# Rebuilding the attention half of a fused relu²-attention and feed-forward kernel on array tiles, with relu on ScalarE and the square on VectorE

## The chip, the cores and the metric

The kernel runs on one core of one Trainium2 chip. The metric is the device time of one execution in microseconds (us). A kernel was run several times; the time quoted is the median. The profile is a record of one execution, and its span is a microsecond or two below the time.

TensorE does matrix products, ScalarE and VectorE bring results out of PSUM (the banks that TensorE writes) into SBUF, GpSimd converts types and issues some of the loads, and SyncE issues the others. In the profile they are PE (PEld for its weight loads), ACT, DVE, POOL and SP.

## The reference

```python
# q, k, v: (8 batches, 12 heads, 448 positions, 64)
scores = q @ k.T / sqrt(64)
attn   = maximum(scores, 0)**2 / 448
x      = (attn @ v) -> (3584 tokens, 768)        # heads side by side
h      = x @ w_in                                # w_in  768 x 2048
out    = maximum(h, 0)**2 @ w_out                # w_out 2048 x 768, out float32
```

The inputs are float32; both kernels compute in fp16 with float32 sums.

## The kernel before

It works through 48 head pairs. For each pair it transposes q and k, computes scores for two heads, applies relu², and multiplies with v. The hidden and output matmuls of earlier batches are kept in a queue, and `fill` puts some of them between the attention matmuls, so that TensorE has work while it waits. A head has only 64 dimensions, but the array is 128 x 128. The kernel pads: q sits in one half of the rows with zeros in the other, and v in one half of the columns with zeros beside it.

```python
ps_p   = tile_pool("ps",   bufs=4, PSUM)   # hidden, scores AND attention-times-V share these
psmi_p = tile_pool("psmi", bufs=2, PSUM)   # transposes
pso_p  = tile_pool("pso",  bufs=1, PSUM)   # output, 768 columns

def relu2_psum_to_sbuf(dst, src, n):            # src is PSUM, read by both engines
    sq = sq_p.tile([P, S], FP16)
    nc.scalar.activation(out=sq[:n], in_=src[:n], func=AF.Square)
    nc.vector.scalar_tensor_tensor(out=dst[:n], in0=src[:n], scalar=0.0, in1=sq[:n],
                                   op0=ALU.is_gt, op1=ALU.mult)     # (src > 0) * sq

# transposes: float32, 4 x 112 rows for q and as many for k, each followed by fill(224)
    nc.tensor.transpose(tq[:, i*SB:(i+1)*SB], qst[:, i], ident)
# ... eviction to qTA (upper half zero), qTB (lower half zero) and kT
# scores: contraction over 128 rows, 64 of them zeros
    for c in range(4):
        for j, qT in ((0, qTA), (1, qTB)):
            nc.tensor.matmul(sps, lhsT=kT[:, c*P:(c+1)*P], rhs=qT, start=True, stop=True)
            relu2_psum_to_sbuf(at, sps, P);  fill(448)
# attention times V: 128 output columns, of which 64 are this head's
    for c in range(4):
        for j in range(2):
            nc.tensor.matmul(avps, lhsT=(vA if j == 0 else vB)[:, c, :], rhs=aa[2*c+j], ...)
            fill(448)
# ... weights are loaded piece by piece, one piece after each head pair of batch 0
```

## Time and profile before

The time was 539.67 us (median of two runs, 539.41 to 539.94).

| what | value | view |
|---|---|---|
| TensorE busy | 498.5 of 538.1 us, 93% | table of busy times |
| VectorE, ScalarE busy | 373.7 us, 297.8 us | table of busy times |
| share of TensorE in the chain that ended last | 87% | chain of waits |
| step of a 448-column matmul | 0.189 us | timeline, start to start |
| third four-head unit's last V matmul | 64.4 us | timeline |

These lines come from the page of the profile before: the span, the busy times of each engine, and three rows that cut the span into 40 equal slices of 13.5 us. A digit is a busy share in tenths; PEclk is the clock that TensorE was granted.

```profile
span 538.1 us, 8018 instructions
...
PE 498.5 (93%) x2816; PEld 281.6 (52%) x2816; DVE 373.7 (69%) x663; ACT 297.8 (55%) x589; POOL 138.5 (26%) x220
...
PE   1675999999999999999999999999999999999886
...
PEclk9979899999999999999999999999999999999999
DMA  9999534544355454343445454343545552100211
```

From the fifth slice on TensorE is at nine tenths or more, until the last three. In the first four the DMA engines are full and TensorE is not. That is batch 0, where the queue has no hidden or output matmuls to fill with.

The next lines are from the timeline of TensorE before, in a dense stretch. The columns are the start (us), the time from the first start to the last end (us), the engine, the line, the operation, output and inputs, the shape of the stationary operand, the shapes of output or moving data, and how many instructions the row joins.

```profile
200.04 0.35 PE L131 MATMUL hps<-xt_119,w_1_97 128*128 128x448 f16 x1
200.23 0.35 PE L236 MATMUL avps<-at_2416,vf_132 128*128 128x448 f16 x1
...
202.69 0.26 PE L217 MATMUL tk<-ident,kst 112*128 112x112 f32 x1
202.79 0.35 PE L131 MATMUL hps<-xt_118,w_0_96 128*128 128x448 f16 x1
...
207.10 0.38 PE L158 MATMUL ops<-w_0_102,g_2451 128*128 128x512 f16 x1
207.31 0.27 PE L162 MATMUL ops<-w_0_102,g_2451 128*128 128x256 f16 x1
207.42 0.35 PE L227 MATMUL sps_2545<-qTA,kT 128*128 128x448 f16 x1
```

Read starts, not durations. A matmul is recorded with 0.35 us, but the next one starts 0.19 us after it (200.04 to 200.23), since they are pipelined. A scores or V matmul with half its rows or columns zero costs the same step as a full one. Averaged over the dense part of the trace, the steps are 0.189 us for 448 columns, 0.215 and 0.109 us for the output pair (512 and 256 columns), and 0.097 us for a float32 transpose.

### The profile page before, as it was taken

Reading aid. Unit: us, or ns where it says so; the run is one execution under the profiler, and the core shown is the slowest. Engines: PE = TensorE matmul, PEld = TensorE weight load, DVE = VectorE, ACT = ScalarE, POOL = GpSimd, SP = SyncE. Lnnn points to the kernel's source line nnn. Section 1 sums busy time; section 2 is a strip of 40 time slices with the busy share of each in tenths; the row PEclk is TensorE's granted clock in tenths of the full one; section 3 lists DMA queues with packets and bytes.
Section 4 is the critical chain, followed back from the end, with each engine's and each line's share of the span. In section 5 each row is a group of like instructions: output and inputs, shape, how many; then the busy total and the mean of one; then the engine's idle time right before and its main releaser. Section 6 shows DMA issues by size and latency. Waiting matters only on the chain.

```text
span 538.1 us, 8018 instructions
## 1 busy us (share of the span) xinstructions
PE 498.5 (93%) x2816; PEld 281.6 (52%) x2816; DVE 373.7 (69%) x663; ACT 297.8 (55%) x589; POOL 138.5 (26%) x220
## 2 busy tenths in 40 slices
PE   1675999999999999999999999999999999999886
PEld 1332455555555555555555555555555555554553
DVE  2676898888887667898875667898875667764000
ACT  0444576667675546676745546676754555654111
POOL 7453311331133122113232123213232113000000
PEclk9979899999999999999999999999999999999999
DMA  9999534544355454343445454343545552100211
GB/s 160 201 204 197 82 51 70 83 84 92 61 86 94 88 119 69 45 78 48 86 85 108 89 120 65 48 75 46 80 93 92 107 108 37 10 0 3 86 60 59
DMA packets 142408, 45.36 MB, mean 84 GB/s; under 512 B 135968, under 2 KB 138016, under 8 KB 142368
## 3 DMA queue, kind: packets, MB, share of 16 engines
q1 hardware_dynamic: 93120, 33.04, 24.9%
q0 software_dynamic: 49248, 11.81, 22.5%
q8 instruction: 22, 0.36, 0.3%
q14 instruction: 18, 0.15, 0.1%
HBM read 45.61 MB, written 11.01 MB: 105 GB/s over the span
## 4 chain that ended last, share of the span: by engine, by line
PE 87%; DMA 7%; ACT 3%; SPq 1%; DVE 1%; issue 1%; ACTq 0%
PE hps L131 27%; PE ops L158 18%; PE avps L236 13%; PE ops L162 9%; DMA kst<-in_k_dram 6%; PE tq L208 3%; PE tk L217 3%; ACT osb L169 2%; DMA qst<-in_q_dram 2%; ACT sq L113 1%; SPq L189 1%; SPq L193 1%; DVE at_527 L114 0%; DVE at_588 L114 0%; DVE at_612 L114 0%
## 5 line engine op out<-in xcount | busy, mean ns | idle before, releaser
L113 ACT ACTIVATE sq<-hps 128x448 f16<-128x448 f32 x128 | 69.4, 542 | 58.2 <-PE hps L131 57.1
L197 POOL DMA_DIRECT2D vf_130<-in_v_dram x24 | 18.4, 768 | 159.6 <-PE avps L236 126.0
L197 POOL DMA_DIRECT2D vf_134<-in_v_dram x24 | 18.4, 768 | 146.3 <-PE avps L236 144.9
L227 PEld LDWEIGHTS <-kT 128*128 128x128 f16 x384 | 36.8, 100 | 32.3 <-issue 4.9
L169 ACT ACTIVATE osb<-ops 128x768 f32<-128x768 f32 x28 | 22.8, 813 | 51.3 <-PE ops L162 51.3
L210 DVE TENSOR_SCALAR qTA<-tq 64x448 f16<-64x448 f32 x48 | 29.2, 608 | 29.6 <-PE tq L208 29.6
L208 PE MATMUL tq<-ident,qst 112*128 112x112 f32 x192 | 33.0, 269 | 15.5 <-DMA qst<-in_q_dram 13.8
L131 PE MATMUL hps<-xt_122,w_4_100 128*128 128x448 f16 x128 | 45.1, 352 | 0.0
L131 PE MATMUL hps<-xt_120,w_2_98 128*128 128x448 f16 x128 | 45.1, 352 | 0.0
L131 PE MATMUL hps<-xt_121,w_3_99 128*128 128x448 f16 x128 | 45.1, 352 | 0.0
L131 PE MATMUL hps<-xt_123,w_5_101 128*128 128x448 f16 x128 | 45.1, 352 | 0.0
L131 PE MATMUL hps<-xt_119,w_1_97 128*128 128x448 f16 x128 | 45.1, 352 | 0.0
L131 PE MATMUL hps<-xt_118,w_0_96 128*128 128x448 f16 x128 | 45.0, 352 | 0.0
L217 PE MATMUL tk<-ident,kst 112*128 112x112 f32 x192 | 35.5, 273 | 8.4 <-DMA kst<-in_k_dram 8.4
L208 PEld LDWEIGHTS tq<-ident,qst 112*128 112x128 f32 x192 | 25.1, 147 | 25.5 <-issue 11.9
L219 DVE TENSOR_SCALAR kT<-tk 128x448 f16<-128x448 f32 x48 | 29.9, 623 | 11.0 <-PE tk L217 9.8
L217 PEld LDWEIGHTS tk<-ident,kst 112*128 112x128 f32 x192 | 25.1, 149 | 15.9 <-issue 10.1
L212 DVE TENSOR_SCALAR qTB<-tq 64x448 f16<-64x448 f32 x48 | 30.1, 628 | 1.5
L131 PEld LDWEIGHTS <-w_5_101 128*128 128x128 f16 x128 | 12.5, 97 | 13.5 <-issue 3.1
L197 POOL DMA_DIRECT2D vf_136<-in_v_dram x24 | 18.7, 779 | 2.9 <-DMA w_5_101<-in_moe_w_in_dram 1.5
L197 POOL DMA_DIRECT2D vf_132<-in_v_dram x24 | 18.8, 782 | 0.0
L131 PEld LDWEIGHTS <-w_2_98 128*128 128x128 f16 x128 | 12.5, 97 | 11.6
(1910 smaller groups left out, 1368.4 us busy)
## 6 DMA issues: line engine op xcount, KB each, us to landing
qst<-in_q_dram SPq DMA_DIRECT2D x96, 112.0 KB, 2.7
kst<-in_k_dram SPq DMA_DIRECT2D x96, 112.0 KB, 2.7
out_dram<-osb SPq DMA_DIRECT2D x28, 384.0 KB, 2.8
vf_130<-in_v_dram POOLq DMA_DIRECT2D x24, 48.0 KB, 2.5
vf_132<-in_v_dram POOLq DMA_DIRECT2D x24, 48.0 KB, 2.9
vf_134<-in_v_dram POOLq DMA_DIRECT2D x24, 48.0 KB, 2.6
vf_136<-in_v_dram POOLq DMA_DIRECT2D x24, 48.0 KB, 2.8
w_0_96<-in_moe_w_in_dram POOLq DMA_DIRECT2D x1, 512.0 KB, 6.1
```

Of the source, the lines that this page charges most:

```text
L113: nc.scalar.activation(out=sq[:n], in_=src[:n], func=AF.Square)
L131: nc.tensor.matmul(hps[0], lhsT=w1[m][:, f * P : (f + 1) * P], rhs=xt[m][:, b * S : (b + 1) * S], start=(m == 0), stop=(m == NDMT - 1),)
L158: nc.tensor.matmul(ops[0][:, 0:512], lhsT=gt[f][:, rs], rhs=w2[f][:, 0:512], start=(f == 0), stop=(f == NFFT - 1),)
L162: nc.tensor.matmul(ops[0][:, 512:768], lhsT=gt[f][:, rs], rhs=w2[f][:, 512:768], start=(f == 0), stop=(f == NFFT - 1),)
L169: nc.scalar.activation(out=osb, in_=ops[0], func=AF.Copy, scale=CO)
L197: nc.gpsimd.dma_start(out=vt[:, 0:3, j * 64 : j * 64 + 64], in_=v[b, 2 * hp + j, 0:384].rearrange("(c p) d -> p c d", p=P),)
L208: nc.tensor.transpose(tq[:, i * SB : (i + 1) * SB], qst[:, i], ident)
L212: nc.vector.tensor_scalar(out=qTB[64:128, :], in0=tq[64:128, :], scalar1=1.0, scalar2=None, op0=ALU.mult)
L217: nc.tensor.transpose(tk[:, i * SB : (i + 1) * SB], kst[:, i], ident)
L219: nc.vector.tensor_scalar(out=kT[:, 0:448], in0=tk, scalar1=SK, scalar2=None, op0=ALU.mult)
L227: nc.tensor.matmul(sps, lhsT=kT[:, c * P : (c + 1) * P], rhs=qT, start=True, stop=True)
L236: nc.tensor.matmul(avps, lhsT=(vA if j == 0 else vB)[:, c, :], rhs=aa[2 * c + j], start=(c == 0 and j == 0), stop=(c == 3 and j == 1),)
```

## The change

Its intent: take the zeros off TensorE, read PSUM once instead of twice for relu², use fewer and larger loads, and keep TensorE's order filled. It is a rebuild. A unit is now four heads (24 units in all), and these are the parts that matter:

```diff
 def relu2(ps, dst):
-    nc.scalar.activation(out=sq, in_=ps, func=AF.Square)          # PSUM
-    nc.vector.scalar_tensor_tensor(out=dst, in0=ps, ... in1=sq)   # PSUM again
+    nc.scalar.activation(out=dst, in_=ps, func=AF.Relu)           # PSUM, fp16 out
+    nc.vector.tensor_mul(dst, dst, dst)                           # SBUF, in place
     (attention: one call for two heads, 896 columns)

 scores: rows 0-63 and 64-127 of the array hold two heads
-    nc.tensor.matmul(sps, lhsT=kT[:, c*P:(c+1)*P], rhs=qT_padded)
+    for j in range(2):
+        r = slice(64*j, 64*j + 64)
+        nc.tensor.matmul(sp[:, j, 0:S], lhsT=kT[r, hp, t*P:(t+1)*P], rhs=qT[r, hp, :])

 attention times V: columns 0-63 and 64-127 hold two heads
+    for hp in range(2):
+        for t in range(3):
+            for j in range(2):
+                nc.tensor.matmul(ap[64*j:64*j+64, hp, 0:S],
+                                 lhsT=vs[:, 4*u+2*hp+j, t*D:(t+1)*D],
+                                 rhs=ats[n, (hp, t)][:, j, :], ...)

 positions 384 to 447 ("tails") of two heads share one full matmul, through
 block-diagonal tiles that are loaded straight from memory:
+    def load_diag(dg, src, b, h0, h1):     # kdg for k, vdg for v, two tiles each
+        for j in range(2): nc.gpsimd.dma_start(out=dg[64*j:..., 64*j:...], in_=src[b, ..., 384:448])

 transposes: float32 -> fp16; GpSimd (VectorE for the first two units) casts q and k
+    eng = nc.vector if n < 2 else nc.gpsimd

 PSUM: -4 shared + 2 transposes + output
       +scores 2 x two banks, hidden and output 2 x one bank,
       +transposes and attention-times-V share one of two banks

 the attention output leaves PSUM through VectorE (before: ScalarE)
 output: 512+256 columns -> 384+384
 weights: eight loads of 1.5 MB instead of 22; the order in the program for GpSimd's queue is
+    kdg(batch 0), v(units of batch 0), w1 x4, w2 x4, then kdg and v of batch 1
 in TensorE's order the transposes of unit n+1 stand between the scores of unit n,
 and the V matmuls of unit n stand after the first scores of unit n+1
```

## The prediction

> **What bounds it now.** TensorE. The busy table gives PE 93%, VectorE 69%, ScalarE 55%; the chain of waits is 87% PE. The timeline of a dense stretch (200 to 212 us) gives true costs as start-to-start steps, not durations: 0.189 us for a 448-column matmul (its record lasts 0.352), 0.215+0.108 for the 512+256 output pair, about 0.10 for a fp32 transpose, or 0.13 in a row. Hidden layer 768 x 0.189 = 145 us, output 448 x 0.324 = 145, scores and attention-times-V 768 x 0.189 = 145, transposes 384 x 0.11 = 42; 477 us of 538. The rest is mostly the start: until about 63 us batch 0 has no filler, DMA is over 90% busy for the first four slices, the table by windows has PE busy 34 of 60 us, and the clock dips to 0.74.
>
> **What the change does.**
> 1. Scores: each padded 128-row matmul (half zeros) becomes one of a pair of 64-row tiles; V matmuls become pairs of 64-column tiles; tails of two heads share one matmul. If the pair runs at once, 384+384 matmuls become 192+192 slots: 145 -> 2 x 37 = 74 us. The Trainium skill (TensorEngine Tiling (Array Packing), Key Properties) says tiles run in parallel and that changing the tiling mode drains TensorE; no trace here shows either.
> 2. Price: about 7 mode changes per four-head unit. A matmul's record outlasts its step by 0.16 us; 0.15 us per change (estimate) gives 168 x 0.15 = 25 us.
> 3. Transposes: fp16, same count, set by the weight load (0.10 us before). Estimate 0.09: 35 us.
> 4. Output is split 384+384, same columns: 896 x 0.1625 = 145 us. Hidden: same.
> 5. ScalarE: 168 relus of 896 columns; from 0.542 us at 448 and 0.813 at 768, about 0.92 each: 154 + hidden 69 + output 27 = 250 us (before 298). VectorE: the square reads only fp16 SBUF; estimate 190 to 230 us (before 374). Both were slack, so this pays only in batch 0.
> 6. Start: packets under 512 B (135,968 of 142,408) mostly become 768 B to 1 KB runs; weights queue behind. First transposes near 9 us, then three units at 7 to 8 us each, held by ScalarE (7 x 0.92) and VectorE, so dense work from about 33 us instead of 63.
>
> **Sum.** 33 start + 21/24 of (74+35) = 95 + mode changes 22 + 290 hidden and output + 15 for waits on the single transposes/AV buffer, for hidden banks behind two 0.92 us relus, and the tail = **455 us** (-16%). Range **436 to 490**. Faster by over 2% 0.96, within 2% 0.03, slower 0.01.
>
> Gain: 30 from the start, 50 from tiling net of mode changes, 5 from transposes, 0 from the relu change.
>
> **What would show it.** Pair starts a few ns apart and 0.19 us per pair (1); a gap of 0.1 to 0.2 us at each change (2); fp16 transposes adding about 0.09 us (3); hidden and output steps as above (4); ScalarE near 250 and VectorE near 210 us, neither on the chain (5); first dense slice near 33 us (6); TensorE still over 85% of the chain.
>
> **What would make it wrong.** Pairs that run one after another (+60 us); mode changes of 0.3 us (+22); GpSimd casts and VectorE squares blocking each other and starving transposes; hidden matmuls queued ahead of scores while the first weights land; PSUM banks, all eight used, making TensorE wait for ScalarE.

## The result

The kernel after took 474.40 us (two runs, 473.24 to 475.57), 12% less. Its output is correct. The ratio to the kernel before is 0.880, with a 95% interval of 0.877 to 0.883. Here and below a ratio is the mean time of one kernel's fast runs over that of the other's in the same rounds, so it is not quite the ratio of the medians that are quoted. 474 lies within the predicted range of 436 to 490, and 19 us above the predicted 455.

The page of the kernel after, the same lines (a slice is 11.8 us here):

```profile
span 473.8 us, 6826 instructions
...
PE 418.6 (88%) x2720; PEld 213.0 (45%) x2720; DVE 215.0 (45%) x380; ACT 237.9 (50%) x353; POOL 90.8 (19%) x145
...
PE   1373159999999999999999999999999999999996
...
PEclk9987569999999999999999999999999999999998
DMA  9999999144804283138504382317001210021022
```

From the seventh slice on TensorE is dense, as before. The start is the surprise: slices one to five show 1, 3, 7, 3, 1 tenths where the kernel before had 1, 6, 7, 5, 9. The clock was granted at 0.5 in the fifth. The DMA engines are full for seven slices instead of four.

The timeline of TensorE after, at the start. What stands in brackets is the idle time in front of the row, and what released it:

```profile
6.85 0.53 PE L270 MATMUL tps<-ident,ks 128*128 128x128 f16 x3
18.69 0.27 PE L270 MATMUL tps<-ident,kdg_91 128*128 128x128 f16 x1 [11.31 <-DMA kdg_91<-in_k_dram]
...
20.70 0.93 PE L297 MATMUL sp<-qT,kT 64*128 64x448 f16 x4 [1.32 <-DVE kT L278]
...
48.25 0.93 PE L261 MATMUL tps<-ident,qs 112*128 112x112 f16 x8 [6.09 <-POOL qs L99]
...
50.33 0.29 PE L270 MATMUL tps<-ident,ks 128*128 128x128 f16 x1
63.61 0.27 PE L270 MATMUL tps<-ident,kdg_95 128*128 128x128 f16 x1 [13.00 <-DMA kdg_95<-in_k_dram]
```

TensorE has little to do until 18.7 us, because the k tails of batch 0 (`kdg_91`, two loads of 48 KB) arrive late: in the trace they are issued after two loads of v (at 3.2 and 3.8 us, after 1.3 and 2.3), although the program names them first. Then it works until 42 us and stops twice more: for the GpSimd casts, and from 50.6 to 63.6 us for the k tails of batch 1 (`kdg_95`).

The timeline of GpSimd after shows that these two stops belong together. Each row is a load that GpSimd issues or a cast that it runs:

```profile
28.01 0.67 POOL L106 DMA_DIRECT2D kdg_95<-in_k_dram  x1 [3.04 <-DMA w_0_137<-in_moe_w_in_dram]
33.86 0.66 POOL L106 DMA_DIRECT2D kdg_95<-in_k_dram  x1 [5.18 <-DMA w_1_139<-in_moe_w_in_dram]
...
46.37 0.66 POOL L106 DMA_DIRECT2D vdg_97<-in_v_dram  x1 [2.86 <-DMA w_0_145<-in_moe_w_out_dram]
47.02 1.18 POOL L99 CAST qs<-qf 112x512 f16<-112x512 f32 x2
```

By the brackets, GpSimd waits for earlier weights to land before it can issue each of these loads, and the casts stand behind the loads in its order. The casts that TensorE waits for at 48.25 us are therefore late because GpSimd was held up issuing the loads of batch 1; each cast itself takes about 0.6 us.

The timeline of TensorE after, in a dense stretch:

```profile
150.41 0.81 PE L227 MATMUL ops<-w_3_151,g 128*128 128x384 f16 x4
151.15 0.55 PE L297 MATMUL sp<-qT,kT 64*128 64x448 f16 x4
151.64 1.32 PE L323 MATMUL avt<-at,vs 128*64 128x448 f16 x12
152.90 0.55 PE L329 MATMUL avt<-at,vdg_93 128*128 128x448 f16 x2
153.28 0.81 PE L227 MATMUL ops<-w_0_145,g 128*128 128x384 f16 x4
...
155.08 0.26 PE L261 MATMUL tps<-ident,qs 112*128 112x112 f16 x2 [0.33 <-DVE xt L333]
```

Twelve V matmuls are spread over 1.32 us, 0.97 us from the first start to the last. The starts within a row, read one by one, come in pairs 3 to 4 ns apart, with 0.189 us from pair to pair (0.213 from the first pair to the second). The four row-tile score matmuls (151.15) come in pairs 3 ns apart too, with 0.200 us between the pairs. The last line shows a stop of 0.33 us. The transposes write the bank that the attention output has just left, so they wait for VectorE to evict it (`xt`).

The waits of TensorE after. The columns are what it did next and what it waited for, total us, times, and the longest:

```profile
PE tps L270 <- DMA kdg_95<-in_k_dram: 13.0, 1, 13.0
PE tps L270 <- DMA kdg_91<-in_k_dram: 11.3, 1, 11.3
PE tps L261 <- POOL ident masks.py:199: 6.2, 1, 6.2
PE tps L261 <- POOL qs L99: 6.1, 1, 6.1
PE tps L261 <- DVE xt L333: 5.8, 20, 0.7
```

The three waits of 13.0, 11.3 and 6.1 us are the ones just seen. The one for `ident` lies before TensorE's first work. The last one is the only large one that comes back in nearly every unit of the dense part (20 waits).

### Where the 65 us came from

I split both traces where the third four-head unit's last V matmul starts. From there on both kernels have nearly all hidden and output work before them (2 of 768 hidden matmuls have started before, 8 after), and about seven eighths of the attention work.

| part | before | after | difference |
|---|---|---|---|
| up to the third unit's last V matmul | 64.4 | 69.5 | +5.1 |
| from there to the end | 473.7 | 404.3 | −69.4 |

A slot is the step of one full matmul or of one pair. The steps read from the traces account for most of the second row. Scores and V went from 768 slots of 0.189 us to 384, of which 7/8 is −63.5 us. The 384 transposes went from 0.097 us to about 0.056 us, of which 7/8 is −13.8. Each change between tiled and full matmuls, or between row and column tiles (a mode change; seven a unit, 168 in all by the program, 175 in the trace), adds 0.096 us (a step of 0.285 instead of 0.189), of which 7/8 is +14.1. The sum is −63.2 of −69.4; the other 6.2 us are not attributed. So the whole gain is in the dense part, and the start lost 5 us instead of gaining about 30.

### The profile page after: what moved, and what is told of

It is laid out like the page before. It is cut to its first block, busy times and chain, and to the rows that moved or that the text cites. A ratio compares the mean times of both kernels' runs of the same rounds, so it can differ in the third digit from the quotient of the medians.

```text
span 473.8 us, 6826 instructions
## 1 busy us (share of the span) xinstructions
PE 418.6 (88%) x2720; PEld 213.0 (45%) x2720; DVE 215.0 (45%) x380; ACT 237.9 (50%) x353; POOL 90.8 (19%) x145
## 5 line engine op out<-in xcount | busy, mean ns | idle before, releaser
L174 ACT ACTIVATE at<-sp 128x896 f16<-128x896 f32 x168 | 146.1, 915 | 106.3 <-PE sp L297 70.3
L175 DVE TENSOR_TENSOR at<-at 128x896 f16<-128x896 f16 x168 | 105.7, 632 | 137.2 <-ACT at L174 137.2
L227 PEld LDWEIGHTS <-g 128*128 128x128 f16 x896 | 82.1, 98 | 51.7 <-issue 2.1
L174 ACT ACTIVATE g<-hps 128x448 f16<-128x448 f32 x128 | 68.7, 546 | 54.0 <-PE hps L189 53.6
L175 DVE TENSOR_TENSOR g<-g 128x448 f16<-128x448 f16 x128 | 55.2, 436 | 46.0 <-ACT g L174 45.9
L261 PE MATMUL tps<-ident,qs 112*128 112x112 f16 x192 | 33.0, 224 | 18.0 <-POOL ident masks.py:199 6.2
L227 PE MATMUL ops<-w_0_145,g 128*128 128x384 f16 x224 | 47.2, 326 | 0.8 <-ACT g L174 0.8
L227 PE MATMUL ops<-w_3_151,g 128*128 128x384 f16 x224 | 47.4, 326 | 0.0
L227 PE MATMUL ops<-w_1_147,g 128*128 128x384 f16 x224 | 47.4, 326 | 0.0
L227 PE MATMUL ops<-w_2_149,g 128*128 128x384 f16 x224 | 46.8, 326 | 0.0
L297 PE MATMUL sp<-qT,kT 64*128 64x448 f16 x288 | 42.5, 371 | 4.6 <-DVE kT L278 3.8
L189 PE MATMUL hps<-xt,w_3_143 128*128 128x448 f16 x192 | 42.2, 352 | 0.9 <-ACT g L174 0.9
L189 PE MATMUL hps<-xt,w_0_137 128*128 128x448 f16 x192 | 42.9, 357 | 0.1
L189 PE MATMUL hps<-xt,w_2_141 128*128 128x448 f16 x192 | 41.8, 352 | 0.0
L189 PE MATMUL hps<-xt,w_1_139 128*128 128x448 f16 x192 | 40.4, 352 | 0.3 <-ACT g L174 0.2
L323 PE MATMUL avt<-at,vs 128*64 128x448 f16 x288 | 35.1, 372 | 1.5 <-DMA w_0_137<-in_moe_w_in_dram 1.4
```

The source lines that it names most:

```text
L174: nc.scalar.activation(out=dst, in_=ps, func=AF.Relu)
L175: nc.vector.tensor_mul(dst, dst, dst)
L189: nc.tensor.matmul(cell[0][:, 0:S], lhsT=w1[f // 4][:, m, (f % 4) * P:(f % 4 + 1) * P], rhs=xt[:, m, :], start=(m == 0), stop=(m == NM - 1))
L227: nc.tensor.matmul(cell[0][:, 0:HALF], lhsT=gt[f][:, tb * P:(tb + 1) * P], rhs=w2[f // 4][:, f % 4, hf * HALF:(hf + 1) * HALF], start=(f = ...
L261: nc.tensor.transpose(cell[0][:, 0, o:o + QP], qs[:, hp, j, :], ident[0:QP, 0:QP])
L297: nc.tensor.matmul(sp[:, j, 0:S], lhsT=kT[r, hp, t * P:(t + 1) * P], rhs=qT[r, hp, :], start=True, stop=True)
```

## The experiments

Two questions were open. One: the prediction put 0 us on the relu change, since VectorE and ScalarE looked slack. Is that so? Two: what holds the start? Theory A is the prediction's own account (the gain is the tiling, and the relu change is worth nothing); theory B, the rival, gives a good part of the gain to relu². Each text says what its theories expect. Ratios are to the kernel before, in the same rounds, with 95% intervals; each kernel in the table had four runs. Differences in microseconds to the kernel after or to s3 are between medians of different rounds. Those of e3 and s1 to the kernel after, and of s8 to s3, are too small to be told from noise: their intervals overlap.

| run | us | ratio | interval |
|---|---|---|---|
| relu change alone in the old kernel (e1) | 540.67 | 1.004 | 1.002–1.005 |
| old relu² in the new kernel (e2) | 502.70 | 0.933 | 0.931–0.935 |
| V matmuls not paired in the order (e3) | 475.82 | 0.883 | 0.882–0.884 |
| scores with padded q (e4) | 483.93 | 0.897 | 0.895–0.900 |
| V matmuls full width, wrong result (e5) | 489.04 | 0.907 | 0.906–0.909 |
| old relu² for attention only (e6) | 478.23 | 0.888 | 0.886–0.891 |
| k tails of batch 0 first (s1) | 475.38 | 0.881 | 0.879–0.883 |
| tails of both first batches early (s3) | 455.46 | 0.845 | 0.843–0.847 |
| s3 + four units cast on VectorE (s5) | 458.45 | 0.851 | 0.849–0.853 |
| s3 + attention output evicted by ScalarE (s6) | 448.79 | 0.833 | 0.831–0.834 |
| s5 + s6 (s7) | 451.89 | 0.838 | 0.837–0.840 |
| s3 + a quarter of the weights, wrong result (s8) | 454.15 | 0.842 | 0.839–0.844 |

### e1: the relu change alone, in the kernel before

```diff
-    nc.scalar.activation(out=sq[:n], in_=src[:n], func=AF.Square)
-    nc.vector.scalar_tensor_tensor(out=dst[:n], in0=src[:n], scalar=0.0, in1=sq[:n], ...)
+    nc.scalar.activation(out=dst[:n], in_=src[:n], func=AF.Relu)
+    nc.vector.tensor_mul(dst[:n], dst[:n], dst[:n])
```

> The old kernel with the relu change alone: ScalarE writes relu in fp16, VectorE squares it from SBUF. Theory A (TensorE's columns and the start bound both kernels; the relu change pays nearly nothing): 533 to 541 us, within 1.2% of before, while VectorE's busy time falls from 374 to about 280 us. Rival B (the relu change, which reads PSUM once, carries much of the gain of 65 us): 520 us or less.

Measured: 540.67 us, no gain. The page of e1:

```profile
span 538.4 us, 8316 instructions
...
PE 503.1 (93%) x2816; PEld 280.6 (52%) x2816; DVE 285.6 (53%) x663; ACT 287.0 (53%) x589; POOL 138.8 (26%) x220
```

VectorE dropped from 373.7 to 285.6 us of work, and the time did not move. So the edit is worth nothing in the old kernel as it was compiled. There is a second thing to see. At 60 us e1 was ahead: 178 matmuls had started against 140 (102 of scores and V against 84), and batch 0 ended at 55.6 us instead of 64.4. The lead was 35 matmuls at 200 us and 3 at 450 us. The mean step from a hidden matmul to a score matmul had grown from 0.213 to 0.225 us. So a gain at the start was given back later; where exactly, I could not settle. The edit also changed the compiled order of TensorE's instructions: read by kind, the two traces differ in 1270 of 2816 places. So e1 doesn't separate the new form of relu² from a new order, and that the form alone would have paid nothing isn't shown.

### e2: the old relu² in the kernel after

```diff
-    nc.scalar.activation(out=dst, in_=ps, func=AF.Relu)
-    nc.vector.tensor_mul(dst, dst, dst)
+    nc.scalar.activation(out=sq, in_=ps, func=AF.Square)
+    nc.vector.scalar_tensor_tensor(out=dst, in0=ps, scalar=0.0, in1=sq, op0=ALU.is_gt, op1=ALU.mult)
 # sq: three buffers; to make room, two output buffers instead of three
```

> The new kernel with the old relu: ScalarE squares, VectorE masks from PSUM, so PSUM is read twice and its banks come free later (output buffers 2 instead of 3 to make room). Theory A: 474 to 486 us; VectorE's busy time rises from 215 to about 310 us. Rival B: 495 us or more, with TensorE waiting for VectorE to free the score and hidden banks.

Measured: 502.70 us, 28 us slower than the kernel after. My theory A fell here. The waits of TensorE in e2 (same columns as above):

```profile
PE hps L196 <- DVE g L179: 10.0, 21, 1.0
PE sp L304 <- DVE at L179: 7.0, 11, 2.3
```

TensorE waits for VectorE, which is busy for only 306 of 502 us. Busy share says nothing here; what counts is when a bank comes free. With the old form a bank is released only once VectorE has read it, and VectorE takes its work in order: in most of the 21 waits the hidden tile stood behind two 896-column attention tiles of 1.08 us each. With the new form ScalarE alone releases it. These listed waits (17 us) are less than 28. The compiled order of TensorE's instructions also changed: by kind it differs from the kernel after in 599 of 2720 places, and the trace of e2 has 260 mode changes instead of 175. At 0.096 us each, the 85 more are an estimated 8 of the 28 us. So part of the price is the order and not the bank.

### e6: the old relu² for the attention tiles only

The edit is e2's, applied where the tile has two heads; the hidden tiles keep the new form. The output buffers are two, as in e2, so this run is also the control for that.

> The old relu for the attention tiles alone; the hidden layer keeps relu on ScalarE and the square from SBUF (2 output buffers as in e2). Theory H (the 28 us of the old relu in the new kernel come from the two hidden banks, which then come free only after VectorE has worked through its queue): 474 to 484 us. Rival (they come from the score banks and from VectorE's load, wherever it stands): 492 us or more.

Measured: 478.23 us. Two waits of e6 answer to those of e2:

```profile
PE sp L306 <- DVE at L181: 6.0, 7, 2.3
...
PE hps L198 <- ACT g L176: 1.1, 5, 0.2
```

The 10.0 us of hidden tiles on VectorE became 1.1 us on ScalarE. Of e2's 28 us, 24.5 come with the old form on the hidden tiles (502.7 − 478.2), and 3.8 with that on the attention tiles and the lost buffer. By the traces the loss of e6 lies at the start: from the third unit's last V matmul to the end e6 takes 404.1 us, the kernel after 404.3 and e2 428.2. The order is not held fixed between the two either: e6 has 192 mode changes, so of the 24.5 us an estimated 6.5 (68 × 0.096) are mode changes. In this kernel hidden and output share two PSUM banks; before, hidden, scores and V shared four. That this is why the same edit was worth nothing in e1 is argued, not tested.

### e3: V matmuls in an order that does not alternate heads

```diff
-        for hp in range(2):
-            for t in range(3):
-                for j in range(2):
+        for j in range(2):
+            for hp in range(2):
+                for t in range(3):
                     nc.tensor.matmul(ap[64*j:64*j+64, hp, 0:S], ...)
```

> The new kernel, with the same V matmuls in another order: all six of the left column tile, then all six of the right, so only one neighbouring pair per unit can overlap. Theory A (two column tiles run at once and TensorE's slots set the time): 11 slots instead of 6 per unit, 5 x 0.189 = 0.95 us for each of some 21 dense units, so 474 + 20 = 490 to 498 us. Rival B, or pairs that gain nothing: 474 to 478 us.

Measured: 475.82 us, only 1.4 us slower. One V group of e3, from its timeline:

```profile
151.08 1.73 PE L323 MATMUL avt<-at,vs 128*64 128x448 f16 x12
```

The starts of those twelve matmuls, in ns from the first one, as the trace has them:

```
0  213  402  408  592  622  781  812  971  1000  1189  1378
```

From 402 ns on these are two streams, each with a step of 0.189 us (0, 213, 402, 592, 781, 971 and 408, 622, 812, 1000, 1189, 1378). The program has six matmuls of one column half, then six of the other; the compiled order has them so in every group but the first. The second half thus started while the first was at its third. In strict order only the sixth and seventh could overlap, and the group would take 10 × 0.189 = 1.89 us; it took 1.38, against 0.97 when paired. So the hardware still overlapped much of the group: taking the pairs out of the order did not take the tiling away, and this run does not price it.

The 0.4 us that each group did lose over 24 groups would be 10 us; only 1.4 appeared. The reason is in the waits. The stop in front of the transposes, waiting for VectorE to evict the attention output, was 5.8 us in 20 waits in the kernel after and 0.7 us in a single one in e3. Added up over units 6 to 18, the steps between V matmuls are 0.41 us a unit longer and the steps into a transpose 0.38 us shorter. The sum, 0.03, is what the period shows (104.54 us for two batches instead of 104.37). So V's loss took the place of a stop that was there before.

### e5: V matmuls at full width (wrong result)

```diff
-    ap[64*j:64*j+64, hp, 0:S], lhsT=vs[:, 4*u+2*hp+j, t*D:(t+1)*D]
+    ap[:, hp, 0:S],            lhsT=vs[:, 4*u+2*hp+j, 0:2*D]
```

> Wrong result on purpose: each V matmul of a pair loads 128 columns (its own and the next 64) and writes all 128 partitions, so no column tiles and no overlap at all: 12 slots instead of 6 per unit, one mode change less. Theory A with a wait (the slots count, but the first transpose behind V's matmuls waits for VectorE's eviction, 0.3 us per unit, and that wait hides part): +1.13 - 0.10 - 0.3 = 0.7 us for each of some 21 units: 484 to 492 us. Rival (column tiles do not matter here, as the reordered run seemed to say): 478 us or less.

Measured: 489.04 us, 14.6 us slower than the kernel after. Without tiles there is nothing to overlap, and two batches (six units, mean of units 6 to 18) take 108.04 us instead of 104.37, which is 0.61 us a unit. The net worth of column tiles is therefore about 15 us. From the steps I would expect more: six slots of 0.189 us are added and one mode change of 0.096 falls away, 1.04 us a unit. The rest is the stop in front of the transposes, as in e3: the steps into a transpose are 0.40 us a unit shorter than in the kernel after.

### e4: scores with padded q in the new kernel

```diff
-    lhsT=kT[r, hp, t*P:(t+1)*P],   rhs=qT[r, hp, :]
+    lhsT=kT[:, hp, t*P:(t+1)*P],   rhs=qpad[n % 2][:, j, hp, :]
 # qpad keeps its zeros; two more copies per unit fill it
 # room: attention tiles 12 -> 11, output buffers 3 -> 2
```

> The new kernel with padded scores: q zero-filled to 128 rows as in the old kernel, no row tiles (11 instead of 12 attention buffers, 2 instead of 3 output buffers, VectorE copies q three times). Theory A: per unit 6 more slots of 0.189 = 1.13 us, less 5 mode changes of 0.096 = 0.48 us, so +0.65 us for each of some 21 dense units: 484 to 492 us. Rival B, or pairs that gain nothing: 470 us or less, as the mode changes alone would go.

Measured: 483.93 us, 9.5 us slower; two batches take 106.55 us, 0.36 us a unit more. The steps alone say 6 × 0.189 − 5 × 0.096 = 0.65. Here too the stop for VectorE's eviction of the attention output goes, from 5.8 us to 0.4. Row tiles are worth this much, net of the extra copies and buffers of the edit. Row and column tiles together are worth about 24 us when taken away singly, against the 50 that I read off the steps (63.5 − 14.1). The two numbers don't measure the same thing. Both runs keep the shared tails, which save four slots a unit, some 16 us by the steps; and each run hid about 5 us of its loss in the stop that the kernel after has. The two kinds of tiles were not removed together.

### s1: the k tails of batch 0 first

```diff
-        nc.vector.memset(kdg_tile, 0.0)
+        nc.gpsimd.memset(kdg_tile, 0.0)   # GpSimd then has no wait before the tail loads
```

> Start, first stall alone: the k tails of batch 0 are loaded first on GpSimd's queue (their zero-fill moves from VectorE to GpSimd, so they need not wait). Theory S (TensorE idles at the start because two small loads of k tails stand behind large ones on one queue: 11 us for batch 0, 13 us for batch 1, and the second lands when it lands): first scores near 11 us instead of 20.7, but the second stall grows by as much, so 466 to 475 us in all. Rival D (the start is as long as the bytes take, whatever their order): 473 to 476 us.

Measured: 475.38 us, no gain. The first scores now start at 14.4 instead of 20.7 us, but the second stop still ends at 64.6 us. The time saved went into the stops behind it: the one for the casts grew from 6.1 to 11.2 us. A stop cured in front of another one only makes the later one longer.

### s3: the tails of batch 0 and of batch 1 early

```diff
 # s1, and
     load_qk(2);  load_v(0, 4, H);  cast_qk(0);  cast_qk(1)
+    load_diag(kdg[1], k, 1, 0, H)
+    load_v(1, 0, H)
     # w1 x4, w2 x4
 ...
-        if u == 0 and b + 1 < B:
+        if u == 0 and 0 < b and b + 1 < B:
             load_batch(b + 1)
```

> Start, both stalls: as s1_kdg_first, and all of batch 1's v and k tails go ahead of the expert weights on GpSimd's queue. Theory S: both stalls (11 + 13 us) go, TensorE is dense from about 40 to 45 us: 450 to 460 us. Rival D (bytes, not order): 468 us or more, as the weights then come later and the hidden layer waits for them.

Measured: 455.46 us, 19 us faster than the kernel after, and by accident the predicted time. The timeline of TensorE in s3, at the start:

```profile
12.52 0.27 PE L272 MATMUL tps<-ident,kdg 128*128 128x128 f16 x1 [4.21 <-DMA kdg<-in_k_dram]
...
14.53 0.93 PE L299 MATMUL sp<-qT,kT 64*128 64x448 f16 x4 [1.32 <-DVE kT L280]
...
31.77 1.30 PE L191 MATMUL hps<-xt,w 128*128 128x448 f16 x3 [4.97 <-DMA w<-in_moe_w_in_dram]
...
48.81 0.55 PE L331 MATMUL avt<-at,vdg 128*128 128x448 f16 x2
...
51.05 0.26 PE L263 MATMUL tps<-ident,qs 112*128 112x112 f16 x2 [1.20 <-DVE xt L335]
```

The two stops for k tails, 11.3 and 13.0 us, are 4.2 us together now. The third unit's last V matmul starts at 49.0 us instead of 69.5, and two batches still take 104.37 us: the dense part did not change. What the start of the kernel after lost was the order of one queue. The k tails of batch 1 were issued at 28.0 and 33.9 us, landed at 61.6 and 63.5, and stood behind eight loads of weights, 12.6 MB in all, the last of which landed at 59.7. The stop of 6.1 us for the casts is gone too: it had come from the same queue. TensorE's order, by kind, is the same in both traces, so s3 changes the loads alone. What is left is a stop of 5.0 us for the first weights. The hidden matmuls that wait for them stand ahead of scores in TensorE's order.

### s5: four units cast on VectorE

```diff
-        eng = nc.vector if n < 2 else nc.gpsimd
+        eng = nc.vector if n < 4 else nc.gpsimd      # on top of s3
```

> s3_both_tails, and VectorE instead of GpSimd casts q and k of units 2 and 3, since GpSimd's queue issues the weight loads ahead of those casts (they ran at 29.8 us). Theory S: the transposes of unit 2 no longer wait, 2 to 5 us less than s3: 450 to 454 us. Rival W (the stretch from 26 to 32 us waits for the first hidden weights, whose matmuls stand ahead in TensorE's order, so that the casts do not matter): 454 to 457 us.

Measured: 458.45 us, 3 us slower than s3. The timeline of VectorE in s5:

```profile
13.70 0.76 DVE L99 CAST qs<-qf 112x512 f16<-112x512 f32 x2 [1.57 <-DMA qf<-in_q_dram]
15.95 0.77 DVE L99 CAST ks<-kf 128x384 f16<-128x384 f32 x2 [1.48 <-DMA kf<-in_k_dram]
18.22 0.76 DVE L99 CAST qs<-qf 112x512 f16<-112x512 f32 x2 [1.50 <-DMA qf<-in_q_dram]
...
21.28 0.62 DVE L278 COPY qT<-tps 128x896 f16<-128x896 f16 x1
```

The casts wait for their loads, and VectorE took its work in order. The eviction of the first unit's q, ready long before, comes at 21.28 us behind casts of units that nobody needs yet. The first scores start at 22.55 us instead of 14.53. The GpSimd casts looked like a culprit (6.1 us in the waits of the kernel after), but s3 has no such wait any more, and moving them made it worse.

### s6: the attention output evicted by ScalarE

```diff
-        nc.vector.tensor_scalar(out=xts[b][:, 2*u:2*u+2, :], in0=ap[:, :, 0:S], scalar1=CX, ...)
+        nc.scalar.activation(out=xts[b][:, 2*u:2*u+2, :], in_=ap[:, :, 0:S],
+                             func=AF.Copy, scale=CX)          # on top of s3
```

> s3_both_tails, and ScalarE instead of VectorE evicts the attention output. Theory E (the 0.3 us that TensorE waits per unit at the first transpose behind V's matmuls is VectorE's eviction, 1.09 us, standing behind two squares of 0.63; ScalarE would be free 0.5 us sooner and takes 0.92): the wait goes, 5 to 8 us less than s3: 447 to 451 us. Rival (the wait only moves to the hidden banks behind ScalarE): 454 to 458 us.

Measured: 448.79 us and correct, 6.7 us faster than s3 and the fastest kernel: 25.6 us below the kernel after, 17% below the kernel before. The page of s6:

```profile
span 446.9 us, 6824 instructions
...
PE 416.1 (93%) x2720; PEld 212.9 (48%) x2720; DVE 191.8 (43%) x354; ACT 258.3 (58%) x377; POOL 93.0 (21%) x147
```

The wait of TensorE for the eviction of the attention output, in s3 and then in s6:

```profile
PE tps L263 <- DVE xt L335: 6.9, 21, 1.2
...
PE tps L263 <- ACT xt L335: 1.0, 2, 0.5
```

ScalarE has 258 us of work for it, VectorE 192. Two batches take 102.57 us instead of 104.37. The bank that transposes and V share comes free sooner, although ScalarE is the busier engine of the two. Two things in the traces say why. ScalarE had stood idle for over 0.15 us before 17 of the 24 evictions, so it could start at once; in s3 VectorE stood idle in 3 of 24, and in the others was still squaring. And the eviction itself took 0.917 us on ScalarE and 1.084 on VectorE (medians).

### s7: s5 and s6 together

> s5 and s6 together. If both theories hold, the gains add: 443 to 449 us; if neither, 454 to 458 us.

Measured: 451.89 us, outside the expected 443 to 449, since s5 was a loss: 3 us slower than s6, which is what s5 cost alone. The period is that of s6 (102.57 us), and the third unit's last V matmul starts at 49.8 instead of 48.5 us. The two effects add up.

### s8: a quarter of the weight loads (wrong result)

The edit loads only the first of the four pieces of each weight matrix, and uses it for all four, on top of s3.

> Wrong result on purpose: s3_both_tails with one of four pieces of each expert weight loaded and used for all. Tells what of the start is bytes: if the first 50 us of s3 are still held by the weight bytes in front of the q and k loads, 440 to 447 us; if only by the order of units without filler (ScalarE and VectorE), 452 us or more.

Measured: 454.15 us, 1.3 us below s3, which the intervals don't separate. One line of the timeline of TensorE in s8:

```profile
35.43 0.93 PE L191 MATMUL hps<-xt,w 128*128 128x448 f16 x2 [6.36 <-DMA w<-in_moe_w_in_dram]
```

Three quarters of the weight bytes are gone, and TensorE still stops 6.4 us at 35 us for the first piece. Once the tails are early, the amount of weights no longer holds the start. What remains would be the order of units, and that no filler exists before batch 0 is done; this was not tested by itself.

## Why the prediction was right, and where it was wrong

The time was right within the range, and the chance put on "faster" (0.96) was borne out. By the prediction's own parts:

1. **Pairs (right).** Pairs start 3 to 4 ns apart, with 0.189 us per pair for V and 0.200 for scores; "0.19 us per pair" was predicted. The Trainium skill (TensorEngine Tiling (Array Packing), Key Properties) says that tiles can run in parallel; the trace agrees.
2. **Mode changes (mechanism right, term too large).** The same section says that a change of mode drains TensorE. What the trace shows fits that: 0.096 us more per change, about the recorded time of one weight load (medians of 0.095 to 0.110), which is 16 us over 168 changes. The prediction had 0.15 and 25.
3. **Transposes (term too large).** 0.056 us or less was measured (steps of 0.048 to 0.056); 0.09 was predicted from the weight load, whose record still has 0.10 us. A weight load is overlapped there, so its record was no floor. The term was 19 us in the dense part instead of 31.
4. **Hidden and output (right).** 0.189 and 0.162 to 0.163 us.
5. **ScalarE and VectorE (busy times right, conclusion wrong).** ScalarE 237.9 (250 predicted), VectorE 215.0 (190 to 230), a relu of 896 columns 0.915 us (0.92). But "0 from the relu change" is wrong in the new kernel: e2 shows 28 us, and e6 that 24.5 of them come with the hidden tiles, through the bank and in part (an estimated 6.5 us) through the order that was compiled. It held in the old kernel (e1), with the same reserve about the order. The prediction inferred from a slack engine that an edit on it is worth nothing; it costed neither the moment at which a bank comes free nor that the new kernel has only two banks for it.
6. **Start (wrong).** The step that failed is "dense work from about 33 us instead of 63". It was 69.5 us. The prediction wrote "weights queue behind", but did not follow that queue to its end: the k tails of batch 1, needed by the fourth unit's transposes, were behind the weights. Those transposes stand in TensorE's order before the third unit's V. "7 to 8 us each, held by ScalarE" failed as well: in s3, without the stops for tails, the three units still take 34.5 us (14.5 to 49.0), and ScalarE is busy for 19.8 of them. Of the 34.5, 5.0 are the stop for weights; the rest was not broken down. The list of risks named two other things (casts, and hidden matmuls queued ahead of scores); they cost 6 us (casts, in the kernel after, held up by GpSimd's load issues and not by VectorE) and 5 us (first hidden weights, seen in s3).

The sum was close because two errors cancelled in part. The start was 36 us too short (33 predicted, 69.5 measured). The rest, 422 predicted and 404 measured, was 17 to 18 us too long, most of it from points 2 and 3 (8 and 12 us over 7/8 of the work). For the waits in the dense part it had 15 us; 404.3 less the terms above (63.5 + 18.8 + 14.1 + 290.7) leaves 17. "TensorE still over 85% of the chain" could not be tested: the chain of the trace after breaks off early, and its shares add up to less than a quarter of the span. s3 supports the account of the start: with the queue put in order the time is 455.5 us, though its third unit still ends at 49.0 and not at 33.

One more check on point 5. VectorE's squares of the hidden tiles (448 columns) had a median of 0.392 us in 101 of 128 cases and of 0.696 (mean 0.612) in the 27 that overlapped a GpSimd cast; in e1, which has no such casts, 0.393. The Trainium skill (SBUF — State Buffer, Who interferes with whom) says that a VectorE instruction with two SBUF inputs contends with GpSimd reading SBUF; the trace agrees. That is 27 × 0.22 = 6 us of VectorE time. The prediction had named it as a risk, and this is its size; what of it reached TensorE was not measured.

## What to carry to other kernels

When loads share a queue, list what each early step of the critical engine needs and where that stands in the queue; small loads of 48 KB in the wrong place of a queue cost more here (19 us, s3) than all mode changes (16). Ask of an eviction not how busy its engine is, but when it frees the bank that TensorE wants next, and try it on the other engine, even a busier one. Read step times from start to start: a recorded duration of a matmul or a weight load is neither its cost nor a lower bound for it.

## What the Trainium skill lacked or had wrong

- TensorE: Matmul & The Clock Gate, Part 3, The mechanism: it says that matmuls start and end in program order. In e3, V matmuls of the second column half start 6 ns after the third of the first half, ahead of three that precede them in the compiled order (twelve starts in 1.378 us, where strict order needs about 1.89). Its 4 ns between tiles agrees (3 to 4 ns).
- The same page, LDWEIGHTS: it gives a time proportional to the columns, columns/1.2 in ns, so 53 for 64 columns. The 128-row, 64-column tile loads here are recorded with a median of 0.110 us (least 0.106), longer than 128 columns with 0.098.
- TensorEngine Tiling (Array Packing), Key Properties: it says that a mode change drains TensorE, but not what that costs. Here it added 0.096 us to a step (0.285 instead of 0.189, 0.258 instead of 0.162).
- TensorE: Matmul & The Clock Gate, Part 4: it gives about 275 ns for a transpose in a kernel. Durations here are near it (0.22 to 0.23 us for one, by the profile), but among other work a fp16 transpose added only 0.048 to 0.056 us to TensorE's time; the page gives no step.
- No page that I read gives the price of a place in a queue: the k tails of batch 1 landed about 30 us after their second issue (33.9 to 63.5 us), behind weights.
